# Two attention layers on one core: an earlier start for part of a query chunk, and a wider choice of the blocks that VectorE exponentiates

## The chip, the core and the metric

One core of a Trainium2 chip runs the whole program. The time is that of the device, in microseconds (us), from the first to the last instruction. All comparisons use runs that were marked as fast.

## The reference

Two layers on 2048 rows of 512 values. Each layer is attention with 32 heads of 16 values, then a dense block with ReLU (512 to 1792 to 512), each on a layer-normalised input and added to `x`. (The code is shortened.)

```python
def _A_ref(x, wqkv, wo):                    # attention; x is layer-normalised
    qkv = (x @ wqkv).reshape(B, S, 3, H, Dh).transpose(2, 0, 3, 1, 4)
    q, k, v = qkv[0], qkv[1], qkv[2]
    scores = jnp.einsum("bhqd,bhkd->bhqk", q, k) * (Dh ** -0.5)
    p = _softmax(scores, axis=-1)
    o = jnp.einsum("bhqk,bhkd->bhqd", p, v)
    return o.transpose(0, 2, 1, 3).reshape(B, S, D) @ wo
...
x = x + _A_ref(_layernorm(x), A_wqkv, A_wo)
x = x + _B_ref(_layernorm(x), B_w1, B_w2)   # and both once more
```

A layer needs 32 x 2048 x 2048 exponentials. They set the time: ScalarE's exponentials are 80% of the chain that ended last in the kernel before.

## The kernel before

A Python scheduler, part of the kernel, writes the instruction order of every engine. In the traces each engine goes through its list in that order: a step that is ready stands behind one that still waits (VectorE, 3.30 us before 1160.57 us, below). Words used below:

- A **chunk** is 512 query rows (layer 2 splits its last one in two). A **segment** is four heads of one chunk against a range of key rows. A **block** is one head's scores of 128 keys by 512 queries.
- A **slot** is three blocks. ScalarE exponentiates all three (a *wide* exponential, 1536 columns), or two (a *narrow* one, 1024) while VectorE computes the third. VectorE works on pairs of such blocks, from two slots.

```python
now = [x for us in banked for x in us]
...
ex = nc.scalar.activation(out=eb[:, 0 : place[m]], in_=b[:, 0 : place[m]], func=ACTF.Exp,
                          scale=1.0 / (LOG2E * UNIT))
...
if half is not None:                 # the third block of this slot is VectorE's
    dve_block(half, taken, b[:, place[m] : W * QS], ex, recent)
```

VectorE's chain for a pair is two reads of scores and five steps on both blocks together (bits, two polynomial steps, the product, bits).

Which segment gives the block. A segment marked `busy` (4 key blocks, that is a short one) gives none:

```python
elif len(pairs) < 2 and ("k", mine["l"], 0 if mine["l"] else 3, NQS - 1) in made:
    ...
    if now_dve[0] + waiting < now_pe[0] + BACKLOG:
        if not mine["busy"] and ends < now_pe[0] + left_here * QS * 0.84 - 1300.0:
            half, take = 0, mine
        elif (left_here < 40 and later and not later["busy"] ...):
            half, take = 0, later
```

Layer 2's first chunk begins with key rows 0 to 1535, since rows 1536 to 2047 come from layer 1's last chunk, whose dense block is still being computed. Its partial sums are stored, and eight short segments finish it:

```python
steps = [(range(4), 0, NKB - TPC), (range(4), NKB - TPC, NKB)]     # layer 2, chunk 0
```

Where a segment ends, its sums are normalised: VectorE copies them to `u`, a transfer gathers 64 values per row group to `c`, VectorE takes reciprocals, a transfer spreads them to `r`, VectorE multiplies to `ot`. The scheduler assumes 3 us for the first transfer and 9.5 us for the second, and there are three buffers of each kind (`NU = 3`):

```python
if n >= NU:
    run_until(("m", n - NU))         # put the older product into the order now
...
nc.sync.dma_start(out=c, in_=sums);  mark(("c", n), lag=3000.0)
...
nc.vector.reciprocal(out=c, in_=c);  ...;  mark(("r", n), lag=9500.0)
```

TensorE repeats score matmuls as **filler** to stay active, up to a floor and up to the time at which the scores are needed (with part of it left out the granted clock was at half for 51 us in e12 and 79 us in e13, against 7 and 0 with it, below):

```python
spare = int(max(need_by - pe_start("s", s_ready), 0.0) / MM)
short = FLOOR * 1330.0 - level - busy[0] - MM * (1 + (len(pend) > held))     # FLOOR = 0.56
times = 1 + min(spare, max(0, math.ceil(short / MM)))
```

The softmax here doesn't subtract the row's maximum and nothing guards it: scores larger than these inputs give would overflow.

Of the kernel before, what the change touches and what calls it, by code (L numbers as in the profile page):

```python
# [12 lines left out]
BF16 = mybir.dt.bfloat16  # L13
# [9 lines left out]
def kernel(  # L23
# [11 lines left out]
    P = 128  # L35
# [4 lines left out]
    H = 32  # L40
# [5 lines left out]
    NKB = S // P  # L46
    NDC = D // P
    QS = 512
    NQS = S // QS
    TPC = QS // P  # L50
    NT = 8
# [23 lines left out]
    AHEAD = (8.0, 8.0)  # L75
    LATE = 0.0
    MID = 2
    FIRST_K = {1: (1, 2, 3), 2: (), 3: ()}
    OWED = 0.0
    SPREAD = 1.3  # L80
# [7 lines left out]
    def sb(shape, dt, name):  # L88
        return persist.tile(shape, dt, name=name)
# [16 lines left out]
            for T in range(4)  # L106
        ],
    ]
    va2 = [sb([P, 2, H // 2, PW], BF16, f"vaug0_{n}") for n in range(2)]
    vaug = [  # L110
        [va2[kb // 2][:, kb % 2] for kb in range(4)]
        + [sb([P, H // 2, PW], BF16, f"vaug0_{kb}") for kb in range(4, NKB)]
    ]
    vaug.append(
        [sb([P, H // 2, PW], BF16, f"vaug1_{kb}") for kb in range(NKB - TPC)] + vaug[0][NKB - TPC :]
# [575 lines left out]
    def add_run(l, j, T, kbs, load=None, store=None):  # L691
        n = len(runs)
        runs.append((l, j, T))
        for e in range(2):
            segs.append(
                {
                    "l": l, "j": j, "t": 2 * T + e, "e": e, "T": T, "kbs": kbs, "n": n,
                    "load": load[2 * T + e] if load else None,
                    "store": store[2 * T + e] if store else None,
                    "w": columns(l, j)[2], "begun": set(), "left": 4 * len(kbs), "short": bool(load or store), "early": bool(store), "busy": len(kbs) == TPC,  # L700
                }
            )

    for l in range(2):

        if l == 0:
            steps = [(range(4), 0, TPC), (range(MID), TPC, 2 * TPC)]
            steps += [(range(MID), 2 * TPC, NKB), (range(MID, 4), TPC, NKB)]
        else:
            steps = [(range(4), 0, NKB - TPC), (range(4), NKB - TPC, NKB)]  # L710
        for Ts, a, b in steps:
            for T in Ts:
                sums = acc if l else acc0
                add_run(l, 0, T, range(a, b), load=a and sums, store=b < NKB and sums)
        for j in range(1, NQS + l):
            for T in range(4):
                add_run(l, j, T, range(NKB))

    norm_no = [0]
    last_steps = []  # L720

    sums_wait = [0]

    def finish_segment(sg, last):
        l, j, t, e = sg["l"], sg["j"], sg["t"], sg["e"]
        sums_wait[0] += 1
        if sg["store"] is not None:

            def store():
                if sg["load"] is not None:  # L730
                    nc.vector.tensor_add(out=sg["store"], in0=sg["load"], in1=ps_o[:])
                else:
                    nc.vector.tensor_copy(out=sg["store"], in_=ps_o[:])
                mark(("po",))
                sums_wait[0] -= 1

            musts.append((690, now_pe[0] + PE_TO_DVE, store))
            return
        n = norm_no[0]
        norm_no[0] += 1  # L740
        if n >= NU:
            run_until(("m", n - NU))
        u, r, c = ubuf[n % NU], rbuf[n % NU], cbuf[n % NU]
        lane = DH if e == 0 else DH - 1
        width = sg["w"]
        at_column = columns(l, j)[1]
        sums = u[lane : P : 32, 0:width]
        c = c[:, 0 : width // 32]

        def copy():  # L750
            if sg["load"] is not None:
                nc.vector.tensor_add(out=u[:], in0=sg["load"], in1=ps_o[:])  # L752
            else:
                nc.vector.tensor_copy(out=u[:, 0:width], in_=ps_o[:, 0:width])  # L754
            mark(("po",))
            mark(("u", n))
            sums_wait[0] -= 1
            if sg not in segs[-2:]:
                nc.sync.dma_start(out=c, in_=sums)
                mark(("c", n), lag=3000.0)  # L760

        musts.append((155 + 1.045 * width, now_pe[0] + PE_TO_DVE, copy))
        b = before(l, j)
        war = each(chunks[b][1], "o", *b) if b else []

        def mul(a, w):
            nc.vector.scalar_tensor_tensor(  # L767
                out=ot[t][:, at_column + a : at_column + a + w], in0=u[:, a : a + w], scalar=mask[e][:, 0:1],
                in1=r[:, a : a + w], op0=ALU.mult, op1=ALU.mult,
            )  # L770
            for i in range(a // P, (a + w) // P):
                mark(("ot", l, j, t, i))

        def recip():
            nc.vector.reciprocal(out=c, in_=c)
            nc.sync.dma_start(out=sums, in_=c)
            nc.gpsimd.dma_start(  # L777
                out=r[:, 0:width],
                in_=bass.AP(
                    tensor=sums.tensor, offset=sums.offset,  # L780
                    ap=[list(sums.ap[0]), [0, 32], [1, width]],
                ),
            )
            mark(("r", n), lag=9500.0)

        def direct(i):
            if i == 0:
                nc.vector.stream_shuffle(
                    out=r[:, 0:width], in_=u[:, 0:width], mask=[lane] * 32
                )  # L790
            a = i * P
            nc.vector.reciprocal(out=r[:, a : a + P], in_=r[:, a : a + P])
            mul(a, P)

        def direct_all():
            for i in range(width // P):
                direct(i)

        ots = each(width // P, "ot", l, j, t)
        if last:  # L800
            last_steps.append(direct)
        elif sg is segs[-2]:
            task(3100, direct_all, ots + [("m", n)], war + [("u", n)])
        else:
            task(250, recip, [("r", n)], [("c", n)], place=0)
            task(180 + 1.1 * width, lambda: mul(0, width), ots + [("m", n)], [("r", n)] + war)
        if t == NT - 1 and not last:
            work.extend(rest_of_chunk(l, j))

    pend = deque()  # L810
# [38 lines left out]
    def pairs_for(sg):  # L849
        return [p for p in pairs if p["sg"] is sg]  # L850
# [165 lines left out]
    wide[0] = False  # L1016
    seen = set()
    level = 0.0
    recents = [[], []]
    now_pe[0] = 12000.0  # L1020
    now_dve[0] = 13400.0
# [6 lines left out]
    while units:  # L1028
# [17 lines left out]
        half = None  # L1046
        if len(banked) == W and pair_at in (None, no):
            mine = banked[-1][0][0]
            left_here = sum(x[0][0] is mine for x in itertools.islice(units, 64))
            later = next((x[0][0] for x in itertools.islice(units, 70) if x[0][0] is not mine), None)  # L1050
            if pair_at == no:
                half, take = 1, pairs[-1]["sg"]
            elif len(pairs) < 2 and ("k", mine["l"], 0 if mine["l"] else 3, NQS - 1) in made:
                queued = sum(t["cost"] for t in dve_q if "chain" in t)
                waiting = sum(t["cost"] for t in dve_q if at(t["deps"], "dve") is not None)
                others = sum(
                    t["cost"] for t in dve_q
                    if "chain" not in t and at(t["deps"], "dve") is not None
                )
                ends = max(now_dve[0] + others, now_pe[0] + 2600.0) + SPREAD * (queued + 5200.0)  # L1060
                if now_dve[0] + waiting < now_pe[0] + BACKLOG:
                    if not mine["busy"] and ends < now_pe[0] + left_here * QS * 0.84 - 1300.0:
                        half, take = 0, mine
                    elif (
                        left_here < 40 and later and not later["busy"]
                        and later["l"] == mine["l"] and not pairs_for(later)
                        and at([("q", later["n"])], "pe") is not None
                    ):
                        half, take = 0, later
            if half is not None:  # L1070
                other = [pairs[-1]["blocks"][0][4]] if half else []
                of_take = [x for x in banked if x[0][0] is take]
                if of_take:
                    x = next((x for x in of_take[::-1] if x[0][2] not in other), of_take[-1])
                    banked.remove(x)
                else:
                    units.appendleft(banked.pop())
                    x = take_unit(heads(banked) + other, take)
                    for sg, kb, g in x:
                        run_until(("k", sg["l"], sg["T"], kb // TPC))  # L1080
                banked.append(x)
                pair_at = no + 2 if half == 0 else None
# [220 lines left out]
```

## Time and profile before

| | before |
|---|---|
| time, median of 3 (range) | 1769.53 us (1769.52 to 1769.78) |
| ScalarE / TensorE / VectorE busy | 97% / 91% / 76% |
| exponentials: wide / narrow | 1076 / 290 |
| granted TensorE clock | 0.998 |

The busy shares say who is occupied, the digits over 40 slices say when, the chain says what the end waited for. The prediction shows these lines and works with them. One number recurs below, the **late starts**: for each exponential, the time to the next one's start, less 1.330 us (wide) or 0.910 us (narrow); summed, it is the time by which ScalarE ran slower than its own pitch. It was read from the trace start by start.

### The profile page before, as it was taken

Reading aid. Unit: us, or ns where it says so; the run is one execution under the profiler, and the core shown is the slowest. Engines: PE = TensorE matmul, PEld = TensorE weight load, DVE = VectorE, ACT = ScalarE, POOL = GpSimd, SP = SyncE. Lnnn points to the kernel's source line nnn. Section 1 sums busy time; section 2 is a strip of 40 time slices with the busy share of each in tenths; the row PEclk is TensorE's granted clock in tenths of the full one; section 3 lists DMA queues with packets and bytes.
Section 4 is the critical chain, followed back from the end, with each engine's and each line's share of the span. In section 5 each row is a group of like instructions: output and inputs, shape, how many; then the busy total and the mean of one; then the engine's idle time right before and its main releaser. Section 6 shows DMA issues by size and latency. Waiting matters only on the chain.

```text
span 1769.2 us, 34798 instructions
## 1 busy us (share of the span) xinstructions
PE 1602.8 (91%) x15093; PEld 518.6 (29%) x15289; DVE 1340.4 (76%) x2045; ACT 1724.3 (97%) x1386; POOL 53.5 (3%) x105
## 2 busy tenths in 40 slices
PE   8898889999999989999989998989998999999998
PEld 2222222222222222222222222222222222444454
DVE  7437788898898888898732244988888888898884
ACT  6999999999999999999999999999999999999994
POOL 0000000000000000000000000000000000000000
PEclk9999999999999999999999999999999999999999
DMA  4001000110002000020001002111100110102112
GB/s 149 1 7 19 15 14 14 37 26 14 8 19 43 15 13 14 17 43 17 9 6 39 4 2 38 20 21 34 26 20 11 28 34 20 22 16 45 26 35 66
DMA packets 110937, 44.54 MB, mean 25 GB/s; under 512 B 98816, under 2 KB 106752, under 8 KB 110784
## 3 DMA queue, kind: packets, MB, share of 16 engines
q1 hardware_dynamic: 92192, 24.38, 5.9%
q0 software_dynamic: 17248, 16.63, 5.0%
q8 instruction: 119, 1.95, 0.5%
q10 hardware_dynamic: 1344, 1.31, 0.2%
q14 instruction: 34, 0.28, 0.1%
HBM read 22.54 MB, written 2.10 MB: 14 GB/s over the span
## 4 chain that ended last, share of the span: by engine, by line
ACT 80%; PE 7%; issue 2%; DVE 2%; DMA 0%; ACTq 0%
ACT e L1131 80%; PE ps_s L1122 3%; PE ps_o L816 2%; PE ps_f L406 1%; PE ps_s L1197 1%; DVE di L862 0%; DMA c<-u 0%; PE ps_f L1197 0%; DVE dy L893 0%; DVE q L567 0%; DVE u L754 0%; DVE de L893 0%; DVE u L752 0%; DVE x L647 0%; DVE dm L887 0%
## 5 line engine op out<-in xcount | busy, mean ns | idle before, releaser
L1131 ACT ACTIVATE e<-ps_s 128x1536 bf16<-128x1536 f32 (+1 forms) x1366 | 1713.9, 1481 | 5.9 <-PE ps_s L1122 5.1
L1122 PE MATMUL ps_s<-q,ktp 32*128 32x512 bf16 (+1 forms) x8081 | 765.0, 357 | 123.7 <-ACT e L1131 98.5
L816 PE MATMUL ps_o<-e,vaug 128*32 128x512 bf16 (+1 forms) x4274 | 428.2, 363 | 5.9 <-DVE u L754 3.0
L1122 PEld LDWEIGHTS <-ktp 32*128 32x128 bf16 x8081 | 236.2, 92 | 613.7 <-issue 515.1
L862 DVE TENSOR_SCALAR di<-ps_s 128x512 int32<-128x512 f32 x290 | 199.4, 687 | 105.1 <-PE ps_s L1122 102.4
L816 PEld LDWEIGHTS <-vaug 128*32 128x32 bf16 x5276 | 139.8, 94 | 294.6 <-issue 273.0
L893 DVE SCALAR_TENSOR_TENSOR dy<-dm 128x1024 f32<-128x1024 f32 x145 | 177.2, 1222 | 3.5
L893 DVE SCALAR_TENSOR_TENSOR dy<-dy,dm 128x1024 f32<-128x1024 f32 x145 | 176.2, 1215 | 2.8
L893 DVE SCALAR_TENSOR_TENSOR de<-dy,di 128x1024 bf16<-128x1024 f32 x145 | 175.9, 1213 | 1.8
L406 PE MATMUL ps_f<-xn2T,w 128*128 128x512 bf16 (+1 forms) x390 | 114.0, 368 | 5.6 <-DVE ht L619 2.3
L619 DVE TENSOR_SCALAR ht<-ps_f 128x512 bf16<-128x512 f32 x105 | 72.2, 687 | 49.9 <-PE ps_f L406 39.9
L406 PE MATMUL ps_f<-w,ht 128*128 128x512 bf16 x339 | 105.3, 384 | 4.2 <-issue 3.8
L816 PE MATMUL ps_o<-de,vaug 128*32 128x512 bf16 (+1 forms) x668 | 101.3, 353 | 4.7 <-DVE u L752 2.3
L887 DVE TENSOR_SCALAR di<-di 128x1024 int32<-128x1024 int32 x145 | 99.8, 689 | 2.3
L777 POOL DMA_DIRECT2D r<-u x70 | 51.1, 730 | 1664.9 <-DMA u<-c 452.2
L887 DVE TENSOR_SCALAR dm<-di 128x1024 int32<-128x1024 int32 x145 | 100.6, 694 | 1.1
L406 PE MATMUL ps_f<-xnT,wqkv 128*128 128x512 bf16 (+1 forms) x266 | 81.3, 371 | 4.6 <-issue 1.4
L567 DVE TENSOR_SCALAR q<-ps_f,qmask 128x512 bf16<-128x512 f32 (+1 forms) x90 | 59.7, 696 | 17.1 <-PE ps_f L406 16.6
L406 PE MATMUL ps_f<-wo,ot 128*128 128x512 bf16 x207 | 65.7, 384 | 2.7 <-issue 2.1
L816 PE MATMUL ps_o<-di,vaug 128*32 128x512 bf16 (+1 forms) x334 | 67.0, 362 | 0.3 <-DVE di L887 0.3
L767 DVE SCALAR_TENSOR_TENSOR ot<-u,mask,r 128x512 bf16<-128x512 f32 (+2 forms) x74 | 49.6, 671 | 14.3 <-DMA r<-u 14.2
L406 PEld LDWEIGHTS <-w 128*128 128x128 bf16 x448 | 33.2, 97 | 81.9 <-issue 73.0
(85 smaller groups left out, 532.3 us busy)
## 6 DMA issues: line engine op xcount, KB each, us to landing
w<-in_B_w_dram SPq DMA_DIRECT2D x126, 128.0 KB
r<-u POOLq DMA_DIRECT2D x56, 256.0 KB, 7.1
out_dram<-x SPq DMA_DIRECT2D x16, 128.0 KB
x<-in_A_x_dram SPq DMA_DIRECT2D x14, 128.0 KB
w<-in_B_w_dram SPq DMA_DIRECT2D x1, 1792.0 KB
r<-u POOLq DMA_DIRECT2D x14, 128.0 KB, 4.6
wqkv<-in_A_wqkv_dram ACTq DMA_DIRECT2D x2, 512.0 KB
c<-u SPq DMA_DIRECT2D x56, 8.0 KB
```

The costliest lines, as they stand in the source:

```text
L406: nc.tensor.matmul(out, lhsT, rhs, start=i % k == 0, stop=i % k == k - 1)
L567: return nc.vector.tensor_scalar(out=qbuf[n % 2][e][:, 0:w], in0=b, scalar1=qmask[e][:, 0:1], scalar2=None, op0=ALU.mult,)
L619: nc.vector.tensor_scalar(out=htp[ft // 2][:, ft % 2 : ft % 2 + number, a : a + w], in0=b.rearrange("p (f q) -> p f q", f=number), scalar1 ...
L767: nc.vector.scalar_tensor_tensor(out=ot[t][:, at_column + a : at_column + a + w], in0=u[:, a : a + w], scalar=mask[e][:, 0:1], in1=r[:, a ...
L777: nc.gpsimd.dma_start(out=r[:, 0:width], in_=bass.AP(tensor=sums.tensor, offset=sums.offset, ap=[list(sums.ap[0]), [0, 32], [1, width]],),)
L816: nc.tensor.matmul(ps_o[32 * g : 32 * g + 32, 0 : sg["w"]], vaug[sg["l"]][kb][:, 4 * sg["T"] + g, 2 * e : 2 * e + 32], rhs, start=g not in ...
L862: first = nc.vector.tensor_scalar(out=di[:, half, :].bitcast(I32), in0=src, scalar1=EXP_BIAS, scalar2=0.0, op0=ALU.add, op1=ALU.max,)
L887: nc.vector.tensor_scalar(out=out[:].bitcast(I32), in0=di[:].bitcast(I32), scalar1=keep, scalar2=put, op0=ALU.bitwise_and, op1=ALU.bitwise_or,
L893: nc.vector.scalar_tensor_tensor(out=out[:], in0=x[:], scalar=c, in1=y[:], op0=ALU.add, op1=ALU.mult)
L1122: nc.tensor.matmul(b[:, a : a + sg["w"]], kt[32 * g : 32 * g + 32, kc : kc + P], qbuf[sg["n"] % 2][sg["e"]][32 * g : 32 * g + 32, 0 : sg[" ...
L1131: ex = nc.scalar.activation(out=eb[:, 0 : place[m]], in_=b[:, 0 : place[m]], func=ACTF.Exp, scale=1.0 / (LOG2E * UNIT),)
L1197: uses(nc.tensor.matmul(out, lhsT, rhs, start=first, stop=last), b, needs=needs)
```

## The change

The intent is to fill the hole in VectorE's work at the start of layer 2 (885 to 1106 us), by three parts: four segments of the second chunk also begin on rows 0 to 1535 (`NEXT`); pairs may begin before layer 2's last keys exist if the dense work is slow enough (`PAIR_PACE`); blocks may come from the current segment or the next two (`FAR = 3`), short segments included.

```diff
+    FAR = 3
+    NEXT = 2
+    PAIR_PACE = 2
...
-            steps = [(range(4), 0, NKB - TPC), (range(4), NKB - TPC, NKB)]
+            steps = [(0, range(4), 0, NKB - TPC), (1, range(NEXT), 0, NKB - TPC)]
+            steps += [(0, range(4), NKB - TPC, NKB), (1, range(NEXT, 4), 0, NKB)]
+            steps += [(1, range(NEXT), NKB - TPC, NKB)]
+            steps += [(j, range(4), 0, NKB) for j in range(2, NQS + 1)]
...
-            elif len(pairs) < 2 and ("k", mine["l"], 0 if mine["l"] else 3, NQS - 1) in made:
+            elif len(pairs) < 2 and (("k", mine["l"], 0 if mine["l"] else 3, NQS - 1) in made or mine["l"] and pace < PAIR_PACE):
...
-                    if not mine["busy"] and ends < now_pe[0] + left_here * QS * 0.84 - 1300.0:
-                        half, take = 0, mine
-                    elif (
-                        left_here < 40 and later and not later["busy"]
...
+                    for n, sg in enumerate(segs[first : here + FAR]):
+                        till = sum(x is sg or segs.index(x) < segs.index(sg) for x in ahead)
+                        if (
+                            sg["l"] == mine["l"] and ahead.count(sg) + (sg is mine) > 1
+                            and at([("q", sg["n"])], "pe") is not None
+                            and ends < now_pe[0] + till * QS * 0.84 - 1300.0
+                        ):
+                            half, take = 0, sg
+                            break
```

Cut: more of layer 1's value tiles are laid in pairs, to hold the four new partial sums, and a chunk's dense work starts when its eighth segment has ended, whichever that is.

More of the change, by code (lines that the diff above doesn't have):

```diff
@@ L108 @@
     ]
-    va2 = [sb([P, 2, H // 2, PW], BF16, f"vaug0_{n}") for n in range(2)]
+    va2 = [sb([P, 2, H // 2, PW], BF16, f"vaug0_{n}") for n in range((NKB - TPC) // 2)]
     vaug = [
-        [va2[kb // 2][:, kb % 2] for kb in range(4)]
-        + [sb([P, H // 2, PW], BF16, f"vaug0_{kb}") for kb in range(4, NKB)]
+        [va2[kb // 2][:, kb % 2] for kb in range(NKB - TPC)]
+        + [sb([P, H // 2, PW], BF16, f"vaug0_{kb}") for kb in range(NKB - TPC, NKB)]
     ]
@@ L706 @@
         if l == 0:
-            steps = [(range(4), 0, TPC), (range(MID), TPC, 2 * TPC)]
-            steps += [(range(MID), 2 * TPC, NKB), (range(MID, 4), TPC, NKB)]
-        else:
-            steps = [(range(4), 0, NKB - TPC), (range(4), NKB - TPC, NKB)]
-        for Ts, a, b in steps:
-            for T in Ts:
-                sums = acc if l else acc0
-                add_run(l, 0, T, range(a, b), load=a and sums, store=b < NKB and sums)
-        for j in range(1, NQS + l):
-            for T in range(4):
-                add_run(l, j, T, range(NKB))
+            steps = [(0, range(4), 0, TPC), (0, range(MID), TPC, 2 * TPC)]
+            steps += [(0, range(MID), 2 * TPC, NKB), (0, range(MID, 4), TPC, NKB)]
+            steps += [(j, range(4), 0, NKB) for j in range(1, NQS)]
+        else:
+            steps = [(0, range(4), 0, NKB - TPC), (1, range(NEXT), 0, NKB - TPC)]
+            steps += [(0, range(4), NKB - TPC, NKB), (1, range(NEXT, 4), 0, NKB)]
+            steps += [(1, range(NEXT), NKB - TPC, NKB)]
+            steps += [(j, range(4), 0, NKB) for j in range(2, NQS + 1)]
+        for j, Ts, a, b in steps:
+            for T in Ts:
+                sums = acc[8 * j :] if l else acc0
+                add_run(l, j, T, range(a, b), load=a and sums, store=b < NKB and sums)
     norm_no = [0]
+    ended = {}
     last_steps = []
@@ L806, in finish_segment @@
             task(180 + 1.1 * width, lambda: mul(0, width), ots + [("m", n)], [("r", n)] + war)
-        if t == NT - 1 and not last:
+        ended[l, j] = ended.get((l, j), 0) + 1
+        if ended[l, j] == NT and not last:
             work.extend(rest_of_chunk(l, j))
@@ L1018 @@
     level = 0.0
+    pace = 0.0
     recents = [[], []]
@@ L1048 @@
             mine = banked[-1][0][0]
-            left_here = sum(x[0][0] is mine for x in itertools.islice(units, 64))
-            later = next((x[0][0] for x in itertools.islice(units, 70) if x[0][0] is not mine), None)
             if pair_at == no:
                 half, take = 1, pairs[-1]["sg"]
-            elif len(pairs) < 2 and ("k", mine["l"], 0 if mine["l"] else 3, NQS - 1) in made:
+            elif len(pairs) < 2 and (("k", mine["l"], 0 if mine["l"] else 3, NQS - 1) in made or mine["l"] and pace < PAIR_PACE):
                 queued = sum(t["cost"] for t in dve_q if "chain" in t)
@@ L1061 @@
                 if now_dve[0] + waiting < now_pe[0] + BACKLOG:
-                    if not mine["busy"] and ends < now_pe[0] + left_here * QS * 0.84 - 1300.0:
-                        half, take = 0, mine
-                    elif (
-                        left_here < 40 and later and not later["busy"]
-                        and later["l"] == mine["l"] and not pairs_for(later)
-                        and at([("q", later["n"])], "pe") is not None
-                    ):
-                        half, take = 0, later
+                    here = segs.index(mine)
+                    first = max(here, segs.index(pairs[-1]["sg"])) if pairs else here
+                    ahead = [x[0][0] for x in itertools.islice(units, 64 + 2 * 64)]
+                    for n, sg in enumerate(segs[first : here + FAR]):
[7 more added lines that the diff above has]
+                            break
             if half is not None:
```

## The prediction

> **What bounds the kernel now.** I began with the page: the busy shares, then the 40 slices, then the chain that ended last.
>
> ```profile
> PE 1602.8 (91%) x15093; PEld 518.6 (29%) x15289; DVE 1340.4 (76%) x2045; ACT 1724.3 (97%) x1386; POOL 53.5 (3%) x105
> ...
> DVE  7437788898898888898732244988888888898884
> ACT  6999999999999999999999999999999999999994
> ...
> ACT 80%; PE 7%; issue 2%; DVE 2%; DMA 0%; ACTq 0%
> ACT e L1131 80%; PE ps_s L1122 3%; PE ps_o L816 2%; PE ps_f L406 1%; PE ps_s L1197 1%; DVE di L862 0%; DMA c<-u 0%; PE ps_f L1197 0%; DVE dy L893 0%; DVE q L567 0%; DVE u L754 0%; DVE de L893 0%; DVE u L752 0%; DVE x L647 0%; DVE dm L887 0%
> ```
>
> The reader is to see three things. ScalarE is busy in every slice but the first and the last, and the exponential (line 1131) alone is 80% of the chain. VectorE is at 8 tenths or more nearly everywhere, but has two holes: slices 2 to 4 (layer 1 starting) and slices 21 to 25, about 885 to 1106 us, where layer 2 starts on rows 0 to 1535. And every slot of three 512-column score blocks is one exponential of 1536 columns, or of 1024 when VectorE computes the third block. So the time is: ScalarE's start, 1366 slots, and a serial tail. The only lever is how many blocks VectorE takes.
>
> Next, the groups kept apart by shape, ScalarE only, in two stretches of 176 us: 885 to 1061 (in the hole), then 1194 to 1370 (dense):
>
> ```profile
> L1131 ACT ACTIVATE e<-ps_s 128x1536 bf16<-128x1536 f32 x131 | 176.5, 1660 | 0.2
> L1131 ACT ACTIVATE e<-ps_s 128x1024 bf16<-128x1024 f32 x2 | 2.2, 1110 | 0.0
> ...
> L1131 ACT ACTIVATE e<-ps_s 128x1536 bf16<-128x1536 f32 x105 | 149.3, 1556 | 0.0
> L1131 ACT ACTIVATE e<-ps_s 128x1024 bf16<-128x1024 f32 x40 | 45.6, 1140 | 0.0
> ```
>
> There is no idle time in either, but the mean durations overlap (131 x 1.66 is more than 176), so the cost of one must come from the pitch. With a for a wide and b for a narrow slot: 131a + 2b = 176 and 105a + 40b = 176. Subtracting, 26a = 38b; so **b = 0.910 us, a = 1.330 us, and a block given to VectorE saves 0.420 us**. Start-to-start medians in the trace, 1.330 and 0.913, confirm it.
>
> Check on the whole: the first exponential starts at 17.9 us and the last ends at 1737.3, so the stretch is 1719.4 us. 1076 x 1.330 + 290 x 0.910 = 1695.0. The remaining **24.4 us** are small late starts. Only 5.9 us of them appear as idle time, since a late start first eats the overlap. After the last exponential come 31.9 us of tail.
>
> Last, the busy time of each engine in the hole and in a dense stretch, 221 us each:
>
> ```profile
> 885.00:1106.00 221.00, 196.14 (x1682) 57.28 (x1702) 76.20 (x145) 219.87 (x166) 4.19 (x7) 1.00 0.09 18
> 1194.00:1415.00 221.00, 201.62 (x1764) 57.60 (x1789) 189.23 (x254) 220.99 (x181) 5.42 (x8) 1.00 0.11 24
> ```
>
> After start and length the columns are PE, weight loads, VectorE, ScalarE, GpSimd. VectorE goes from 76 us to 189 us with ScalarE still gapless, so 86% of VectorE can be used without hurting. The hole holds about 113 us unused.
>
> [...]
>
> **The change part by part.** I compared the instruction orders of the two programs (no times in them).
>
> *ScalarE.* Both have 1366 exponentials. The narrow ones rise from 290 to 338, the wide ones fall by the same 48. Per 40 slots, from slot 680 to 839 (the hole), before has 0, 0, 2, 0 narrow ones and after has 10, 10, 12, 12: 42 more. The rest is +5 in slots 80 to 159, and ups and downs of one to three. So 48 x 0.420 = **20.2 us off ScalarE's path**, 17.6 of it in the hole.
>
> *How it comes about.* Three parts work together. (1) Layer 2's second chunk begins on rows 0 to 1535 for four segments (a segment is four heads; 48 blocks each here, so 64 slots of about 1.2 us), before chunk 0 needs rows 1536 to 2047. The dense layers of the last chunk of layer 1 thus have some 64 slots more to finish; their matmuls in slots 680 to 839 fall from 228 to 182 in the order. (2) Pairs may start in layer 2 before its last keys exist, if the filler pace is under 2 groups a slot. (3) Blocks may come from up to three segments ahead. For the share of each I counted edited programs, not run: without (2), 292 narrow ones; without (1), 322; without both, 312; with a reach of two segments, 340. No part adds up alone.
>
> *VectorE.* Per pair: 2 x 0.687 + 0.694 + 1.222 + 1.215 + 1.213 + 0.689 = 6.41 us. 24 more pairs are 154 us. Two more runs add 4 query masks (0.74 each), 4 stored partial sums (0.69), and 4 final copies become adds of the same cost: 5.7 us. So VectorE's busy time goes to about 1340 + 160 = **1500 us**, 86% of 1750. That is the dense level everywhere. Weighting the instructions between VectorE's score reads by these durations gives 44 to 47 us for each 40 slots of the old hole (20 to 21 before), the same as in the dense stages (42 to 50): full, not fuller.
>
> *TensorE.* Score matmuls 8081 to 7817 (fewer fillers), value matmuls 5276 to 5376 (a pair needs three passes where the exponential's output needs two for two blocks), projections +8. Fewer in all, and the hole's dense-layer load is thinned. TensorE stays beside ScalarE, where it waits for scores to be read: it costs nothing.
>
> *Buffers.* Four more partial sums lie in layer 1's value tiles, whose last readers end before layer 2. No wait that matters.
>
> *Sum.* 1769.5 - 20.2 = 1749.3. The late starts, read slot by slot from the trace as start-to-start less 1.330 or 0.913: the four 40-slot windows of the hole have 2.4 us now, dense windows have about 0.75 each, so about +1; and VectorE is a little fuller at other places, another +1. **Prediction 1751 us, 1.0% faster.**
>
> **Rivals.** *VectorE becomes the bound.* Its chain of a pair then ends late, value matmuls wait in order behind it, score matmuls behind them, and ScalarE starves. For it: VectorE loses its slack in the hole just where layer normalisation and evictions of the last chunk feed layer 2's last keys. Against it: the dense stage lives with the same load, and blocks from further ahead are needed later. If each of 24 pairs lost 0.3 us, 7 us of the gain would go: 1757.
> *The last keys come late.* A stall near 1080 to 1110 us, since VectorE now does two jobs there. Against: 64 slots, about 75 us, of extra lead. One stall of 5 us would make 1756; the opposite, late starts falling below today's, could give 1746.
> *More than arithmetic.* Over 2% faster needs 35 us; 20.2 plus all 24.4 us of late starts would be needed nearly whole. I see no mechanism.
> *Nothing gained, as the work was hidden.* Against: ScalarE is gapless in the hole, so narrower exponentials shorten it directly.
>
> **Range and chances.** The count of blocks is certain and the cost of one is measured, so the spread is the late starts: from -5 to +6 us. I give 1746 to 1757 for 8 in 10. Slower by 2% would need a stall of 55 us: 0.02. Faster by 2%: 0.02.
>
> **What would show it.** Right: 338 exponentials of 1024 columns; VectorE at 8 or more tenths in slices 21 to 25; its busy time near 1500 us; ScalarE's pitch unchanged at 1.33 and 0.91; TensorE's clock still 1.00; the tail still about 32 us. Wrong: idle time of ScalarE near layer 2's last keys; value matmuls waiting for the last VectorE steps; late starts well over 30 us in sum.

## The result, and the profile after

The changed kernel takes **1759.03 us** (median of 4, 1757.28 to 1760.61) against 1769.65 us before. Ratios here are the mean of one kernel's fast runs over the mean of the other's in the same rounds, so not quite the ratio of the medians: 0.994 (95% interval 0.9922 to 0.9957). That is 10.6 us, where 18.5 were predicted, and just above the range of 1746 to 1757.

The page of the kernel after: busy shares, then VectorE's and ScalarE's busy tenths in the 40 slices, then the shares of the chain.

```profile
PE 1603.6 (91%) x14939; PEld 523.5 (30%) x15133; DVE 1482.0 (84%) x2221; ACT 1705.6 (97%) x1386; POOL 54.8 (3%) x105
...
DVE  7438988888998999899789989879889888889884
ACT  6999999999999999999999999989999999999994
...
ACT 84%; PE 11%; DVE 2%; issue 2%; DMA 1%; ACTq 0%
```

The hole is gone: slices 21 to 25 now read 8, 9, 9, 8, 9. But ScalarE, at 9 before in all slices but the first and the last, has an 8 in slice 27, about 1143 to 1187 us. The busy time in the old hole, and in the stretch after it (columns as in the prediction: TensorE, weight loads, VectorE, ScalarE, GpSimd):

```profile
885.00:1106.00 221.00, 204.96 (x1724) 60.00 (x1749) 199.61 (x282) 220.01 (x180) 0.00 (x0) 1.00 0.04 10
1115.00:1165.00 50.00, 38.94 (x366) 11.60 (x373) 35.19 (x51) 46.51 (x37) 4.06 (x6) 1.00 0.17 30
```

In the hole VectorE does 200 us where it did 76, ScalarE is busy for 220.0 of the 221 us, and runs 180 instructions where it ran 166. In the 50 us from 1115 ScalarE loses 3.5 us outright.

Where did the gain go? The start of one and the same slot in the two profiled runs, in us:

| slot | before | after | lead |
|---|---|---|---|
| 80 | 125.0 | 125.4 | -0.3 |
| 680 (layer 2 begins) | 870.6 | 868.0 | 2.6 |
| 840 (end of the hole) | 1084.9 | 1065.1 | 19.8 |
| 920 | 1185.7 | 1170.5 | 15.2 |
| 1360 (end) | 1729.9 | 1719.0 | 10.9 |

**At slot 840 the whole gain is there.** It is then given back: 4.6 us within 80 slots, and 4.3 us over the remaining 440. The account of the whole span: nominal ScalarE work fell by 20.2 us as counted (1693.7 to 1673.5), late starts rose by 9.1 (25.0 to 34.1), start and tail by 0.6. The sum is -10.5, and the spans differ by 10.4.

Most of the 4.6 us lie where the eight short segments of chunk 0 end, called the **closing stage** below: 50 slots, 875 to 924 in the new order, 811 to 860 in the old. First VectorE's waits of the kernel before in its closing stage, 1050 to 1105 us (who waited for whom: total us, times, longest):

```profile
DVE c L775 <- DMA c<-u: 15.8, 6, 5.2
DVE u L752 <- PE ps_o L816: 9.7, 3, 5.3
DVE ot L767 <- DMA r<-u: 7.2, 2, 4.1
```

Then of the kernel after, 1115 to 1165 us:

```profile
DVE di L869 <- PE ps_s L1132: 4.3, 4, 1.5
DVE c L781 <- DMA c<-u: 3.3, 1, 3.3
DVE ot L773 <- DMA r<-u: 3.3, 2, 2.1
DVE u L758 <- PE ps_o L823: 2.4, 2, 2.1
```

VectorE waited for the transfers of the sums far longer *before*: 23 us, against 6.6 us. But before, the closing stage had 1.8 us of late starts, and after it has 5.8. The timeline of the kernel after shows why for the largest piece (start, duration, instruction, and in brackets the idle time before it and what ended it):

```profile
1154.25 0.54 SPq L765 DMA_DIRECT2D c<-u  x1
...
1160.57 0.25 DVE L781 RECIPROCAL c<-c 128x16 f32<-128x16 f32 x1 [3.30 <-DMA c<-u]
1160.74 1.16 DVE L900 SCALAR_TENSOR_TENSOR de<-dy,di 128x1024 bf16<-128x1024 f32 x1
...
1161.94 0.69 DVE L894 TENSOR_SCALAR di<-di 128x1024 int32<-128x1024 int32 x1
1162.55 0.74 DVE L570 TENSOR_SCALAR q<-ps_f,qmask 128x512 bf16<-128x512 f32 x1
...
1163.21 0.68 DVE L758 TENSOR_TENSOR u<-vaug,ps_o 128x512 f32<-128x512 f32 x1
...
1163.94 0.40 PE L823 MATMUL ps_o<-e,vaug 128*32 128x512 bf16 x4 [2.92 <-DVE u L758]
...
1164.49 0.47 PE L1132 MATMUL ps_s<-q,ktp 32*128 32x512 bf16 x3
...
1165.00 1.02 ACT L1141 ACTIVATE e<-ps_s 128x1024 bf16<-128x1024 f32 x1 [2.17 <-PE ps_s L1132]
```

The gather of the sums is issued at 1154.25 and its reciprocal starts at 1160.57, 6.3 us later; the scheduler had counted on 3. VectorE stands still 3.3 us *in order*. Behind the reciprocal there are now two exp steps and a query mask before the copy of `ps_o`. TensorE waits 2.9 us for that copy, the next scores come late, and ScalarE idles 2.17 us. Before the change mostly sums and query masks stood behind such waits, and most of the waits cost nothing. One did cost something, the longest:

```profile
1096.48 0.25 DVE L775 RECIPROCAL c<-c 128x16 f32<-128x16 f32 x1 [5.20 <-DMA c<-u]
1096.65 1.32 DVE L567 TENSOR_SCALAR q<-ps_f,qmask 128x512 bf16<-128x512 f32 x2
...
1098.20 4.80 ACT L1131 ACTIVATE e<-ps_s 128x1024 bf16<-128x1024 f32 x4 [0.85 <-PE ps_s L1122]
```

Two query masks stood behind it, and ScalarE was 1.2 us late. So the waits were there all along; the change put exponential steps behind them too, ahead of the copy that TensorE needs.

Slot by slot, the 5.8 us of the closing stage after are: 1.5 at slot 905 (the next scores waited for query masks, and these for their projection: no transfer), 2.4 at slot 915, the stall shown, 1.4 in the two slots behind it, while the TensorE clock was at half for 3.4 us, and 0.5 in small pieces.

### The profile page after: what moved, and what is told of

Read it like the earlier page. It is cut to its first block, busy times and chain, and to the rows that moved or that the text cites. A ratio compares the mean times of both kernels' runs of the same rounds, so it can differ in the third digit from the quotient of the medians.

```text
span 1758.8 us, 34642 instructions
## 1 busy us (share of the span) xinstructions
PE 1603.6 (91%) x14939; PEld 523.5 (30%) x15133; DVE 1482.0 (84%) x2221; ACT 1705.6 (97%) x1386; POOL 54.8 (3%) x105
## 4 chain that ended last, share of the span: by engine, by line
ACT 84%; PE 11%; DVE 2%; issue 2%; DMA 1%; ACTq 0%
ACT e L1141 84%; PE ps_s L1132 4%; PE ps_o L823 3%; PE ps_f L409 2%; PE ps_s L1207 1%; DVE dy L900 0%; DMA c<-u 0%; DVE di L869 0%; DVE stats L438 0%; PE ps_f L1207 0%; PE ps_s L968 0%; DMA x<-in_A_x_dram 0%; DVE ht L622 0%; DVE q L570 0%; PE ps_s L477 0%
## 5 line engine op out<-in xcount | busy, mean ns | idle before, releaser
L1141 ACT ACTIVATE e<-ps_s 128x1536 bf16<-128x1536 f32 (+1 forms) x1366 | 1695.2, 1456 | 13.4 <-PE ps_s L1132 12.4
L1132 PE MATMUL ps_s<-q,ktp 32*128 32x512 bf16 (+1 forms) x7817 | 746.2, 357 | 118.6 <-ACT e L1141 91.3
L869 DVE TENSOR_SCALAR di<-ps_s 128x512 int32<-128x512 f32 x338 | 232.3, 688 | 94.0 <-PE ps_s L1132 91.2
L823 PEld LDWEIGHTS <-vaug 128*32 128x32 bf16 x5376 | 144.9, 94 | 301.3 <-issue 277.6
L900 DVE SCALAR_TENSOR_TENSOR dy<-dm 128x1024 f32<-128x1024 f32 x169 | 206.4, 1221 | 3.8
L900 DVE SCALAR_TENSOR_TENSOR dy<-dy,dm 128x1024 f32<-128x1024 f32 x169 | 205.7, 1217 | 2.7
L900 DVE SCALAR_TENSOR_TENSOR de<-dy,di 128x1024 bf16<-128x1024 f32 x169 | 205.1, 1214 | 1.7
L894 DVE TENSOR_SCALAR dm<-di 128x1024 int32<-128x1024 int32 x169 | 116.6, 690 | 0.9
L823 PE MATMUL ps_o<-de,vaug 128*32 128x512 bf16 (+1 forms) x768 | 114.7, 358 | 2.2 <-DVE vaug L739 0.8
L894 DVE TENSOR_SCALAR di<-di 128x1024 int32<-128x1024 int32 x169 | 115.2, 681 | 1.7
```

What stands on the lines that cost most here:

```text
L823: nc.tensor.matmul(ps_o[32 * g : 32 * g + 32, 0 : sg["w"]], vaug[sg["l"]][kb][:, 4 * sg["T"] + g, 2 * e : 2 * e + 32], rhs, start=g not in ...
L869: first = nc.vector.tensor_scalar(out=di[:, half, :].bitcast(I32), in0=src, scalar1=EXP_BIAS, scalar2=0.0, op0=ALU.add, op1=ALU.max,)
L894: nc.vector.tensor_scalar(out=out[:].bitcast(I32), in0=di[:].bitcast(I32), scalar1=keep, scalar2=put, op0=ALU.bitwise_and, op1=ALU.bitwise_or,
L900: nc.vector.scalar_tensor_tensor(out=out[:], in0=x[:], scalar=c, in1=y[:], op0=ALU.add, op1=ALU.mult)
L1132: nc.tensor.matmul(b[:, a : a + sg["w"]], kt[32 * g : 32 * g + 32, kc : kc + P], qbuf[sg["n"] % 2][sg["e"]][32 * g : 32 * g + 32, 0 : sg[" ...
```

## The experiments

Seventeen kernels were run, and the changed kernel once more, all with correct results, five rounds each. The late starts are those of each run's profile (one execution, which need not be the median one); "closing" is the closing stage, "waits" VectorE's idle time there (and up to 2 us behind it) that a transfer ended, "half" the time at half TensorE clock between 20 and 1735 us.

| run | median us | ratio to before | narrow | late, all | closing | waits | rest | half |
|---|---|---|---|---|---|---|---|---|
| before | 1769.5 | | 290 | 25.0 | 1.8 | 23.4 | 23.2 | 0 |
| after | 1759.0 | 0.9940 | 338 | 34.1 | 5.8 | 6.5 | 28.3 | 7 |
| r1 after again | 1759.0 | 0.9936 | 338 | 37.8 | 10.6 | 6.6 | 27.2 | 17 |
| e1 no short | 1759.4 | 0.9938 | 326 | 29.2 | 2.9 | 23.0 | 26.4 | 3 |
| e2 lag | 1768.7 | 0.9993 | 342 | 38.7 | 1.8 | 4.3 | 36.8 | 3 |
| e3 floor 0.60 | 1767.3 | 0.9986 | 342 | 42.5 | 3.1 | 1.5 | 39.4 | 7 |
| e4 no early start | 1774.0 | 1.0018 | 322 | 41.8 | 16.2 | 8.1 | 25.6 | 17 |
| e5 no pace rule | 1776.6 | 1.0034 | 292 | 33.3 | 6.0 | 4.9 | 27.3 | 7 |
| e6 look-ahead alone | 1765.5 | 0.9969 | 312 | 29.6 | 5.8 | 4.3 | 23.8 | 14 |
| e7 old choice | 1768.3 | 0.9989 | 306 | 31.7 | 5.7 | 21.5 | 26.0 | 7 |
| e8 local lag | 1766.4 | 0.9980 | 342 | 44.5 | 13.9 | 5.9 | 30.7 | 20 |
| e9 lag, ring of 4 | 1757.2 | 0.9924 | 338 | 32.3 | 2.1 | 1.5 | 30.2 | 0 |
| e10 reach 2 | 1766.6 | 0.9976 | 340 | 42.3 | 9.3 | 5.0 | 33.0 | 20 |
| e11 floor 0.50 | 1749.0 | 0.9876 | 342 | 27.1 | 2.3 | 2.9 | 24.8 | 10 |
| e12 less filler | 1757.0 | 0.9925 | 338 | 34.6 | 6.1 | 6.4 | 28.5 | 51 |
| e13 before, less filler | 1781.3 | 1.0064 | 290 | 38.2 | 2.0 | 21.8 | 36.2 | 79 |
| e14 before, floor 0.50 | 1770.9 | 1.0002 | 290 | 25.6 | 2.0 | 22.0 | 23.6 | 17 |
| e15 floor 0.45 | 1754.4 | 0.9914 | 342 | 29.3 | 0.6 | 2.3 | 28.7 | 3 |
| e16 narrow, no filler | 1768.6 | 0.9995 | 338 | 42.2 | 4.6 | 6.1 | 37.5 | 61 |
| e17 both remedies | 1754.1 | 0.9911 | 342 | 30.5 | 0.8 | 0.7 | 29.7 | 14 |

The 95% intervals of the ratios reach 0.0012 to 0.0018 to either side, so kernels whose ratios lie closer than some 0.002 are not told apart: after, r1, e1, e9 and e12 among them. And "closing" mixes two things. In r1, e4, e8 and e10, 8.6, 7.8, 10.8 and 8.2 us of it fell in slots that ran while the clock was at half for some of the time; in after, e1 and e7 it was 3.8, 2.5 and 3.9, in before, e9, e15 and e17 nothing.

Theories: **A**, VectorE's in-order waits in the closing stage; **B**, VectorE is near its ceiling everywhere and the loss is scattered; **C**, too little filler, so the clock halves; later **F**, filler that ends at the deadline makes TensorE late after a narrow slot.

### The changed kernel again (r1_after_again)

> The changed kernel once more, for a second profile and more times. Nominal ScalarE work: 338 narrow slots, so late starts in the profiled run = stretch of the exponentials less 1027 x 1.330 + 338 x 0.910. First profile: 35 us of late starts, of them 5.8 in slots 880 to 919, and two half-clock spells of 3.4 us. Theory A (a local stall where chunk 0's short segments end, VectorE's in-order wait for the sums' transfer): 5 to 6 us there again. Theory B (VectorE is near its ceiling everywhere and late starts are spread): 34 to 36 in all, another place worst. Theory C (fewer filler matmuls, so the clock falls to half by chance): runs with clock 0.998 take 1757, each further 0.001 of clock costs 1.7 us. Median 1759 in all three.

The stall returned at the same slots: 905 and 915 are late by 1.5 and 3.0 us here, by 1.5 and 2.4 in the first profile. The place belongs to the instruction order, not to chance. What is chance is what follows: in the first profile the clock fell to half for 3.4 us after the stall (at 1164.7 us), here for 17.1 us from within the stall (at 1161.6 us), which makes 10.6 of late starts. The rest, 27 to 28 us, repeats. So A holds for the place of the larger stall and C for the variation; the medians of both measurements agree (1759.03, 1759.04).

### No blocks from the short segments (e1_no_short)

```diff
-                            sg["l"] == mine["l"] and ahead.count(sg) + (sg is mine) > 1
+                            not sg["busy"] and sg["l"] == mine["l"] and ahead.count(sg) + (sg is mine) > 1
```

> VectorE takes no blocks from the short last-row segments of chunk 0 in layer 2 (as before the change): 326 narrow slots instead of 338, which costs 12 x 0.42 = 5.0 us of ScalarE. Theory A: the late starts of slots 840 to 919 fall from 7 to about 2, so the time stays within 1 us of the changed kernel, 1759. Theory B: late starts fall by at most 2 us, 1762. Theory C: fillers rise from 7817 to 7927, clock a little steadier, 1761.

Twelve narrow slots fewer cost 5.0 us by count, and the time is the same. VectorE's waits in the closing stage, 1110 to 1165 us, are back at the old size:

```profile
DVE c L781 <- DMA c<-u: 15.7, 6, 5.2
DVE u L758 <- PE ps_o L823: 10.2, 5, 5.4
DVE ot L773 <- DMA r<-u: 7.2, 2, 4.2
```

The late starts there are down to 2.9, and 2.5 of these lie in two slots beside a spell at half clock. Twenty-three us of waits cost little where 4 narrow slots stand, and with 6.5 us of waits 5.8 are lost where 11 do. In the kernel as it is, the blocks that the change takes from the short segments are worth nothing net.

### A longer transfer in the scheduler's books (e2_c_lag, e8_lag_local, e9_ring4_lag)

```diff
-                mark(("c", n), lag=3000.0)
+                mark(("c", n), lag=7000.0)                                      # e2
+                mark(("c", n), lag=7000.0 if (l, j) == (1, 0) else 3000.0)      # e8, e9
-            mark(("r", n), lag=9500.0)
+            mark(("r", n), lag=12000.0 if (l, j) == (1, 0) else 9500.0)         # e9
-    ubuf, cbuf: NU = 3 buffers, run_until(("m", n - NU))
+    ubuf, cbuf: NV = 4 buffers, run_until(("m", n - NV))                        # e9
```

(The last pair is shortened; `r` keeps three buffers.)

> The scheduler assumes 7 us instead of 3 us for the transfer of the sums, so the reciprocal stands later in VectorE's order and does not block it while the transfer is under way (342 narrow slots, 4 more: -1.7 us). Theory A: the stall at slots 880 to 919 shrinks from 5.8 to about 1.5 us: 1753. Theory B: only the 4 slots: 1757. Theory C: fillers 7902, 1757.

> The scheduler counts 7 us instead of 3 us for the transfer of the sums, but for layer 2's first chunk alone, so everything before slot 880 stays as in the changed kernel (342 narrow slots, 4 more, all later: -1.7 us). Theory A (VectorE's in-order wait for that transfer costs ScalarE 5 us while the short segments end): late starts of slots 880 to 919 fall from 5.8 to 2 or less, 1753.5. Theory B (scattered): the stage improves less than 2 us, or the loss comes back later; 1757 to 1759.

> As the local 7 us for the sums' transfer, with 12 instead of 9.5 us for the spread of the reciprocals too, and a fourth buffer for sums so that no step is forced early by the ring of three. 338 narrow slots, as in the changed kernel. Theory A: no VectorE wait on a transfer in the stage, late starts there under 2 us, 1755. Theory B: 1759.

e2 did for the closing stage what A said (5.8 to 1.8) and lost it elsewhere, since the books changed for the whole kernel: the rest went from 28 to 37 us. e8, meant to avoid that, was a plain miss: the closing stage got worse, 13.9. Its VectorE timeline, 1136 to 1150 us:

```profile
1137.01 0.24 DVE L781 RECIPROCAL c<-c 128x16 f32<-128x16 f32 x1
...
1144.32 0.75 DVE L773 SCALAR_TENSOR_TENSOR ot<-u,mask,r 128x512 bf16<-128x512 f32 x1 [5.26 <-DMA r<-u]
```

The reciprocal no longer waits. It is later, so its spread is later too; with three buffers the next segment forces the product into the order (read from the code), and VectorE stands 5.26 us for the second transfer. A wait was moved, not removed. That stall makes 6.3 us of late starts in two slots; 4.5 of the rest lie in slots at half clock, most of them in the 17.1 us that began within the stall. e9 also tells the scheduler of the second transfer and adds a fourth buffer. Its waits, 1115 to 1165 us:

```profile
DVE di L870 <- PE ps_s L1133: 6.7, 5, 1.9
DVE u L759 <- PE ps_o L824: 5.3, 3, 4.2
DVE ot L774 <- DMA r<-u: 1.5, 1, 1.5
```

With 1.5 us of transfer waits the closing stage has 2.1 us of late starts instead of 5.8, at the same 11 narrow slots there; the profile has no half-clock spell, and the five runs lie within 2.2 us. The stall at slot 915 and the slow slots behind it, 3.8 us in the changed kernel, are gone; the 1.5 us at slot 905 are still there. At slot 920 e9 stands at 1164.1 us, 6.4 us ahead of the changed kernel (of these, 1.3 come from an earlier first exponential). A is shown for this stall, by the three edits together; which of them was needed was not tried. But the median gained only 1.8 us, within the noise: behind slot 920 the order is another one, and late starts there are 15.1 us against 11.8.

### The parts undone (e4_no_early, e5_no_pace, e6_look_only, e7_old_pick)

e4 sets `NEXT = 0`, e5 sets `PAIR_PACE = 0`, e6 both; e7 puts the old choice of segment back and keeps the other two parts.

> Part 1 undone: no early start of the second chunk; the pace rule and the look-ahead stay. 322 narrow slots, 32 more than before: 13.4 us at 0.42. If late starts stay as before (25 us): 1756. If blocks in chunk 0's short segments (slots 811 to 853 here) stall as in the changed kernel (theory A, 5 us): 1761. If every further narrow slot also loses 0.14 us by scattered late starts (theory B): 1765.

> Part 2 undone: VectorE may begin pairs in layer 2 only when its last keys exist; the early start and the look-ahead stay. 292 narrow slots, as many as before within 2, and none in slots 680 to 839. Count alone: 1768.7. Theory A: blocks in the short segments remain (17 in slots 840 to 919), so the stall of 5 us remains: 1774. Theory B: as before, 1769.

> Parts 1 and 2 undone, the look-ahead alone: 312 narrow slots, 22 more, 9.2 us at 0.42. Count alone: 1760. Theory A (short segments stall, slots 811 to 853): 1765. Theory B (0.14 us lost for each): 1763.

> Part 3 undone: blocks only from the current segment or the next one, none from the short segments, as before; early start and pace rule stay. 306 narrow slots, 40 of them in slots 680 to 839, 6 in slots 840 to 919. 16 more: 6.7 us at 0.42. Theory A (no block in short segments, no stall): 1763, late starts near 25. Theory B: 1765.

By count, e4 should stand 13.4 us ahead of before; it is 0.2% *slower*. Its closing stage comes straight behind the hole and loses 16.2 us. The two largest pieces, 3.9 and 3.8 us, are not waits for a transfer. ScalarE's chain runs back through the query masks and the projection of the last keys, which are made just before the scores that need them; at the second:

```profile
1088.25 0.69 DVE L530 CAST ktp<-ps_f 128x512 bf16<-128x512 f32 x1 [1.11 <-PE ps_f L409]
1089.00 1.25 PE L1132 MATMUL ps_s<-q,ktp 32*128 32x512 bf16 x13 [0.46 <-DVE ktp L530]
...
1089.42 2.37 ACT L1141 ACTIVATE e<-ps_s 128x1024 bf16<-128x1024 f32 x2 [3.61 <-PE ps_s L1132]
```

So the early start is not only room for blocks: with pairs in the hole but without its extra slots, the last keys come late. That is a rival of the prediction, come true in a kernel that lacks part 1. e5, part 2 undone, has 292 narrow slots, practically as before, and is 0.3% slower; closing stage 6.0, of it 2.2 beside one 4.1 us wait for a gather. e6, the look-ahead alone, keeps 5.5 of the 9.2 us counted. e7 missed by 3 to 5 us, and its interval (0.9976 to 1.0001) does not tell it from the kernel before: with no block from the short segments the closing stage still lost 5.7 us. There the pair of the *following* segment ran into it: its timeline has VectorE standing 4.2 us for the second transfer at 1177.7, with the read of the next scores behind it:

```profile
1177.71 0.75 DVE L773 SCALAR_TENSOR_TENSOR ot<-u,mask,r 128x512 bf16<-128x512 f32 x1 [4.20 <-DMA r<-u]
1178.38 0.68 DVE L869 TENSOR_SCALAR di<-ps_s 128x512 int32<-128x512 f32 x1
...
1179.12 0.92 PE L1130 MATMUL ps_s<-q,ktp 32*128 32x512 bf16 x6 [2.78 <-DVE di L869]
```

The next exponential is 3.0 us late, beside 3.4 us at half clock. One block behind one transfer is enough.

### A reach of two segments (e10_far2)

> Reach of two segments instead of three: 340 narrow slots. The instruction order up to slot 919 has the same counts. Theory A: stall in slots 880 to 919 as in the changed kernel, 1758. Theory B: late starts about 35, 1758. It tells whether the third segment of reach is worth anything: no.

`FAR = 2` gives two more narrow slots and loses 7.5 us: 9.3 in the closing stage, with 20 us at half clock (14 of them there). The expectation missed. The third segment's worth is not settled by this: the counts per 40 slots are the same up to slot 919, but the order differs in places from slot 93 on.

### Filler (e3_floor60, e11_floor50, e14_before_floor50, e15_floor45)

`FLOOR` of 0.60, 0.50 and 0.45 in the changed kernel, 0.50 in the kernel before.

> The floor for TensorE's activity raised from 0.56 to 0.60, so fillers are repeated more often (8111 score matmuls, against 7817 after and 8081 before; 342 narrow slots, -1.7 us). Theory C: clock 0.998 in every run, spread of times under 1 us, 1755. Theories A and B: no gain but the 4 slots, 1757, or a loss where fillers delay other matmuls.

> TensorE's activity floor 0.50 instead of 0.56: fewer repeated score matmuls (7169 against 7817), 342 narrow slots. If fillers placed up to the deadline cause the late starts after narrow slots (14.9 us), these fall to 10 or less; if the clock needs the fillers, half-clock spells multiply and the clock falls to 0.99. Theory C: slower, 1765 or more. Theory B with fillers as the cause: 1754.

> The kernel before with the activity floor 0.50 (7120 score matmuls, 290 narrow slots): the partner of the changed kernel's 1749.0 at 0.50. By count alone the difference between the two is 52 x 0.42 = 21.8 us, so 1770.8 if nothing is gained here; theory F says 1764 to 1767 (less filler, fewer late starts); a difference near 20 us at 0.50 would show that the counted gain is real and that 0.56 hid it.

> The changed kernel with the floor at 0.45 (7062 score matmuls, 342 narrow slots). If 0.50 was good by less filler, this is as good or better: 1747 to 1750. If it was good by luck of the order where the short segments end, this falls back to 1755 to 1762. Theory C: clock under 0.995, slower.

More filler (e3) did not steady the clock (0.995 to 0.999), and with its other order the kernel was 8 us slower: C fails as the main cause of the loss. At 0.50 the changed kernel takes **1749.0 us**, 1.2% faster than before and the best of all. Its page:

```profile
PE 1569.5 (90%) x14302; PEld 509.6 (29%) x14493; DVE 1492.4 (85%) x2235; ACT 1702.2 (97%) x1386; POOL 54.3 (3%) x105
```

TensorE is busy 34 us less, and ScalarE's late starts are 27.1 us. The kernel before gains nothing from 0.50 (ratio 1.0002). So at 0.50 the change is worth 0.9876 / 1.0002 = 0.9874, some 22 us, and 52 narrow slots more at 0.42 are 21.8. **Where the order is good, the counted gain arrives in full**: late starts 27.1 against 25.6. But 0.45, with less filler still, falls back to 1754.4, with more late starts behind slot 920 (15.0 us against 11.3; 6.5 in slots 960 to 1039, against 4.4). So 0.50 is one good order, the best of those tried, and not a rule about filler.

### Filler alone, all other order kept (e12_fewer_fill, e13_before_fewer_fill, e16_narrow_no_fill)

```diff
-        for _ in range(times):
+        for rep in range(times):
             pe_run("s", 1, s_ready)
+            if rep and rep == times - 1:          # e12, e13; in e16: if rep and half is not None
+                continue
```

> The changed kernel with its order of all other instructions kept, but the last filler pass of each slot that has one left out (5842 score matmuls instead of 7817; 338 narrow slots; VectorE's and ScalarE's programs the same). Theory F (filler passes that end at the deadline make TensorE late in the next, shorter slot): late starts fall from 34 to 24 or less, 1749. Theory A alone (VectorE's waits for transfers at the end of the short segments): nothing changes but the fillers, late starts 32 to 34, 1758. Theory C (the clock needs them): clock under 0.99, 1765 or more.

> The same for the kernel before: its order kept, the last filler pass of each slot left out (5755 score matmuls instead of 8081; 290 narrow slots). Theory F: fewer late starts here as well, but less, since they follow narrow slots (8.1 us of 25 against 14.9 of 34): 1764 to 1766. If it gains as much as the changed kernel does, fillers do not explain why the change gave less than counted. Theory A: 1769. Theory C: slower.

> The changed kernel, order of all else kept, filler passes left out only in slots whose own exponential is narrow (6987 score matmuls instead of 7817; other slots keep theirs, so the clock should hold at 0.995 or better). Theory F: late starts after narrow slots fall from 14.9 to 9 or less and the time to about 1753. If F is wrong they stay near 15 and the time at 1759. The stage where the short segments end keeps its 5 to 6 us (theory A), since VectorE's order is the same.

In e12 the closing stage keeps its loss (6.1, with slots 905 and 915 late by 1.5 and 2.1 again): filler has no part in A. The late starts after narrow slots fall from 14.9 to 10.9, in e13 only from 8.1 to 7.1: in favour of F, for at most 4 us. But the time hardly moved, as the clock was at half for 51 us, and e13 became 0.6% slower with 79 us at half clock. e16, the cleaner test of F, missed: 13.1 instead of 9 or less, 61 us at half clock, some 9.5 us slower than the changed kernel. Filler does hold the clock here (51, 79 and 61 us at half without these passes, 7, 0 and 7 with them); of F too little is left to build on.

### Both remedies (e17_best)

> The changed kernel with the floor at 0.50 and, for layer 2's first chunk, the longer transfer times and the fourth buffer for sums (342 narrow slots). If both remedies add: late starts about 25, 1747. If the order behind slot 920 is unlucky, as in the run with the buffer alone: 1750 to 1753.

Its closing stage has 0.8 us of late starts, the best but one, and 0.7 of waits, the fewest, and still it is 5 us slower than e11, by 7.1 us of late starts in slots 1000 to 1039, which e11 has at 3.7, and a longer tail. The remedies do not add.

## Why the prediction was wrong

- **The bound.** Right: ScalarE's exponentials are 84% of the chain after.
- **The cost of a block, 0.420 us.** Right: start-to-start medians after are 1.330 and 0.907 us. The durations are longer, since neighbours overlap: before, 1132 and 1575 ns in the mean at start-to-start medians of 913 and 1330 ns.
- **The count, and the hole.** Right: 338 narrow ones; slots 680 to 839 took 197.2 us after and 214.3 before. That is 17.1 us less, where 17.6 less about 1 for late starts, some 16.6, were foreseen.
- **VectorE's busy time, 1500 us.** 1482. The prediction adds up durations, and these rose by 157.7 us in sum (1422.3 to 1580.0) where 160 were foreseen; neighbours overlap, by 81.9 us in all before and 98.0 after, so the busy time rose by 141.6.
- **TensorE "costs nothing".** This failed in single slots. Its busy time in sum is 1603.6 us after and 1602.8 before, but it hands VectorE's waits on to ScalarE (2.92 us at 1163.94, and ScalarE 2.17 us idle at 1165.00), and in a slot with value and dense matmuls it needs longer than a narrow exponential does ("the other 5 us", below).
- **The late starts, "about +1" and "another +1".** This term of the sum failed: it measured +9.1 in the first profile. About 4 of it is the closing stage (1.8 to 5.8; 3.8 of the 5.8 are the stall and two slots at half clock behind it). The prediction looked at how *much* VectorE would work there ("full, not fuller") and asked nothing about the waits that already stood in that stage. The lists of waits of the kernel before had them: 23 us, in six waits for the gather and two for the spread. They cost 1.8 us in all as long as mostly sums and query masks stood behind them in VectorE's order. e9 (same count of blocks there, waits 1.5 us, loss 2.1) and e1 (waits 23, few blocks, loss 2.9) show both halves.
- **The other 5 us** lie in the rest (23.2 to 28.3), and all of them after narrow slots (7.9 to 14.2 there; after wide slots 15.3 to 14.1). Filler can be part of it (e12), but the direct test failed (e16). The trace names the larger part. TensorE's and ScalarE's timelines of the kernel after:

```profile
1253.50 0.39 PE L1132 MATMUL ps_s<-q,ktp 32*128 32x512 bf16 x3
1253.82 0.61 PE L823 MATMUL ps_o<-e,vaug 128*32 128x512 bf16 x6
1254.36 0.60 PE L409 MATMUL ps_f<-xn2T,w 128*128 128x512 bf16 x2
1254.90 0.39 PE L1132 MATMUL ps_s<-q,ktp 32*128 32x512 bf16 x3
...
1255.34 1.45 ACT L1141 ACTIVATE e<-ps_s 128x1536 bf16<-128x1536 f32 x1 [0.24 <-PE ps_s L1132]
```

  From one slot's scores to the next TensorE works 1.40 us without idle time and without filler (three score matmuls are one pass), on value and dense matmuls; the exponential in between is a narrow one, whose pitch is 0.91, so the next starts 0.49 late. Counted over the rest, late starts of more than 0.15 us behind narrow slots with a single pass of scores and no idle time of TensorE: 6 before (1.7 us), 18 after (7.1 us), 18 in r1 (7.0), 10 in e11 (3.6). So in these slots TensorE is the bound, and the rise is about as large as the 5 us. No experiment moved those matmuls alone, so this is read from the traces and **not shown by a run**; why an order has more or fewer such slots stays open. The rest does depend on the order: kernels with 338 to 342 narrow slots have from 24.8 to 39.4 us of it.
- **The rivals.** "VectorE becomes the bound" describes the path of the stall correctly (value matmuls wait, scores behind them, ScalarE starves), but spread over all pairs; it is local. "The last keys come late" named a stall of 5 us, at the wrong place and for the wrong reason: it came at 1154 to 1166 us, from the sums' transfers. Where it did come true is e4, without the early start.
- **The range.** -5 to +6 us for the late starts took today's 25 us as a property of the kernel. It is one of its instruction order: rearranging made 27 to 45 us at nearly equal counts (0 to 20 us at half clock among it).

The clock adds to this. Where its spells at half fall, and how long they last, varies between executions of one program (two of 3.4 us in the first profile of the changed kernel, one of 17.1 us in the second). Three began within or right behind a stall (at 1164.7 us behind TensorE's 2.92 us of idle time from 1161.0; in r1 at 1161.6, within 2.94 us of it; in e8 within the stall of 5.26 us); the other one of the first profile, at 219.2 us, had no idle time of TensorE over 0.52 us in the 6 us before it. In r1, 8.6 of the 10.6 us of late starts in the closing stage fell in slots at half clock, so if the stall is what brought the spell on, which was not tested, it cost more than its own length.

## What to carry to other kernels

When idle time of an engine is to be filled, list its waits in that stretch first: here 23 us of in-order waits cost 1.8 us, and one of 3.30 us left ScalarE idle for 2.17 once exponential steps stood behind it. Look also for slots in which another engine already works without idle time for longer than the shortened step takes (TensorE's 1.40 us beside a pitch of 0.91). A counted gain on the bounding engine is an upper end; in a statically ordered kernel the late starts belong to one order, and a change that rearranges everything should be tried with a few neighbouring settings before it is judged (here 0.56 gave 10.6 us of 20, and 0.50 all of its 22). And a transfer time in a scheduler's books should be the one measured in that stage; corrected for one of two chained transfers alone, it moved the wait (e8).

## What the traces show besides

- In the longest spell at half clock (r1, 17.1 us) TensorE was busy: 15.30 of the 17.00 us from 1161 to 1178, at a granted clock of 0.52. The matmuls agree with the clock: in the first profile of the changed kernel three score matmuls took 0.61 us at 1165.86, within its spell of 3.4 us, and 0.39 at 1151.33, before it. What ends a spell was not tested.
- The gather of 8 KB of sums took 6.3 us from its issue to the start of the waiting reciprocal at 1154 us; in the closing stage of the kernel before, where the reciprocal waited six times, it took 1.8 to 1.9 us three times, 2.3, 3.9 and 5.2. A 256 KB spread had been issued 0.9 us before the gather of 6.3 us, and the three longest ended 0.2 to 0.3 us after a spread had landed. But two of the gathers of 1.8 us (at 1077.85 and 1084.56) also began while a spread was under way, so that the spread held the others up is a guess.
